# Sigmoid attention and mixture of depths on one core: the value matmuls from 32 rows to 64 rows

## The chip, the cores and the metric

The kernel runs on one core of a Trainium2 chip. The metric is device time in microseconds (us) of one execution; the time before is the median of three runs, 455.39 us (454.31 to 455.57). All data is float32.

## The reference

Two blocks follow each other. `q`, `k` and `v` are (8, 12, 448, 64): 8 batches, 12 heads, 448 tokens, 64 dimensions a head. The first block is attention with a sigmoid in place of the softmax; its output, heads side by side, is `x` (8, 448, 768). The second block picks 128 of the 448 tokens of each batch by a gate score and adds a gated two-layer network to those rows alone.

```python
scores = scale * np.matmul(q, k.transpose(0, 1, 3, 2)) - np.log(S)
attn = 1.0 / (1.0 + np.exp(-scores))
return np.matmul(attn, v).astype(np.float32)
...
scores = np.einsum('bsd,d->bs', x, w_gate)
out = x.copy()
for b in range(B):
    top_idx = np.argpartition(-scores[b], capacity)[:capacity]
    xe = x[b, top_idx]
    h = np.maximum(xe @ w1, 0.0)
    ye = h @ w2
    g = 1.0 / (1.0 + np.exp(-scores[b, top_idx]))
    out[b, top_idx] = x[b, top_idx] + g[:, None] * ye
```

`w1` is (768, 1024), `w2` is (1024, 768).

## The kernel before

**Quads, sets and slots.** Four heads of one batch are a quad; there are 24 quads and 12 sets `s` of two quads. The 448 tokens are 14 blocks of 32. A set has seven slots `n`; in slot `n` the keys of blocks `n` and `n + 7` (64 keys) are scored against all 448 queries, for both quads.

**Scores** (`score`, L329 to L341). VectorE has turned `q` and `k` in 32x32 squares, so that head `h` of a quad lies on the 32 partitions from `32 h` on, half of its 64 dimensions at a time (`e`). One matmul contracts 32 rows: the weights are 32x64 (64 keys), the moving operand is 32x448. It uses rows `32 h` of the array and, for quad `y` of the set, column half `y`. `pr` picks heads 0, 1 or heads 2, 3, so one call of `score` uses the lower or the upper two row groups, and both column halves. A pair of heads has its own PSUM tile `PA[pr]`, of two banks. ScalarE turns it into `attn[s, pr, n]` (`squash`, L352): 64 keys of the one quad on partitions 0 to 63, of the other on 64 to 127; the two heads of the pair side by side.

**Values** (`value`, L357 to L371). Here the keys are contracted. Before the change this is done by 32 rows: for quad `half` of a set, row group `2 half` holds one block of 32 keys and row group `2 half + 1` the other, and the output, the 64 dimensions of head `j` of pair `pr`, is added up in the bank `PO[x][pr]`. Two row groups that run at once write to different banks: with `p = 0` the lower row group does pair 0 and the upper one pair 1, with `p = 1` it is the other way round (`pr = r % 2 ^ p`). Each slot's blocks have to be done with both `p`. `rounds` (L717) lists which `p` and which two slots' blocks are done in the place of each slot; where `p` changes within a slot (`split`, L727), `join` (L373) lets ScalarE write one element into the banks between the two parts. In `rest` a `drain` stands between the two `p`.

**A slot** (`slot`, L737). Values lag four slots behind the scores. For `half` 0 and 1, with `pr = 1 - half`: first part of the scores (`e = 0`) of pair `pr`, the values of `half`, second part of the scores (`e = 1`), sigmoid. The scores of a half-slot so use one pair of row groups and its values the other pair. One half-slot before the change has 8 score matmuls and 8 value matmuls in the program; each float32 matmul leaves two weight loads and two matmuls in the trace. A split slot (L752 to L764) has both halves' values, then all scores, then both halves' values.

**Around the attention.** After slot 3 of a set, `after` (L851) brings: `load_v` (the values of a later set, four DMAs, L153), `block` (L679: a piece of the mixture-of-depths network for an earlier batch, as `BLOCKS` lists it, L649), `turn` (VectorE's 32x32 squares for `q` and `k`, L312, L320), `load`, `gates` (VectorE, L396, L399: two products and sums for each quad's part of the gate score). `takes` (L388) moves the finished values out of `PO` with VectorE. In `BLOCKS`, `("c", b)` is the choosing: small matmuls (L481, L485) that make the 128 token numbers of batch `b` out of `ranking` (L444 to L475, VectorE); `(1, p, key)` and `(2, p, key)` are products of the first and the second layer (L559, L623), with seven quarter products instead of eight; `("t", b)` turns the gathered rows (L523). Each item of a block takes its bank from the list `places`, whose first is a score bank and whose second is `PO[0][0]`. `RANKED` (L910) says after which slot a batch's `ranking` comes, `WEIGHTS` (L221) after which slot a quarter of `w1` or `w2` is loaded (768 KB each), `None` standing for the one that is kept in a spare tile.

**Order.** The program order is written out by hand. All loads and stores shown here are issued by SyncE's queue (SP) in that order; the gathers and scatters by GpSimd.

Of the kernel before, what the change touches and what calls it, by code (L numbers as in the profile page):

```python
# [17 lines left out]
def kernel(  # L18
# [11 lines left out]
    nc = tc.nc  # L30

    B, H, S, Dh = q.shape
# [4 lines left out]
    TT = 32  # L37
    TB = S // TT
    NF = 3
# [171 lines left out]
    def keep_sum(m, key):  # L211
# [6 lines left out]
            (6, 6): (2, 5), (7, 0): (2, 6), (7, 4): (2, 7), (7, 5): (2, 4)}  # L218
    KEPT = {(6, 0): [(1, 5), (1, 7)], (6, 1): [(1, 6)], (6, 5): [(1, 3)],
            (7, 0): [(2, 5)], (7, 1): [(2, 6)], (7, 5): [(2, 7)], (7, 6): [(2, 4)]}  # L220
    WEIGHTS = {(1, 2): (1, 0), (1, 5): (1, 1), (2, 1): (1, 2), (2, 2): (1, None),  # L221
               (5, 1): (2, 0), (5, 5): (2, 1), (6, 1): (2, 2), (6, 4): (2, None)}

    def attn_tile(pr, n):
# [129 lines left out]
    x_tiles, gate_parts, st = {}, {}, {}  # L354
    done = {}

    def value(s, half, p, n):  # L357


        for r in (2 * half, 2 * half + 1):  # L360
            x, c, step = chunks(s, n, half)
            pr = r % 2 ^ p
            rows = slice(r * TT, (r + 1) * TT)
            at = column(s, n, half) * Dh
            i = done[s, x, pr] = done.get((s, x, pr), 0) + 1
            for j in range(2):
                nc.tensor.matmul(PO[x][pr][j * Dh:(j + 1) * Dh, :S],  # L367
                                 raw_v[s][rows, 2 * pr + j, at:at + Dh],
                                 attn[s, pr, n][rows, j, :],
                                 start=((s, x, pr, j) not in done), stop=(i == TB))  # L370
                done[s, x, pr, j] = True  # L371

    def join(x):  # L373

# [266 lines left out]
    def scatter(b):  # L641
# [7 lines left out]
    BLOCKS = {  # L649
# [8 lines left out]
    }  # L658
# [20 lines left out]
    def block(s):  # L679

        places = [PA[1][:, 0], PO[0][0], PO[0][1], PA[0][:, 0], PO[1][0], PO[1][1], PA[0][:, 0]]
        work = BLOCKS.get(s, ())
        if work and work[0][0] == "c":
            chosen = choose(work[0][1], places.pop(0))
        takes(s - 1, 0)
        if work and work[0][0] == "c":
            fetch(*chosen)
            work = work[1:]
        takes(s - 1, 1)
        stores(s, NF)  # L690
        if s in FULL:
            gates(2 * s - 2)
        for item in work:
            if item[0] == "t":
                turn_rows(item[1], [places.pop(0) for _ in range(2)])
            elif item[0] == "c":
                fetch(*choose(item[1], places.pop(0)))
            else:
                finish(item, begin(item, places.pop(0)))
# [14 lines left out]
    outs = None  # L714
    FULL = [(NG * b + NG - 1) // 2 + 1 for b in range(B)]

    def rounds(s):  # L717


        if s == 0:  # L720
            return [(0, 0, 1), (1, 0, 1), (1, 0, 1), (0, 0, 1), (0, 4, 5), (0, 1, 6), (1, 4, 5)]
        same = [(0, 0, 1), (1, 0, 1), (1, 2, 3), (0, 2, 3), (0, 4, 5)]
        if s + 1 in BLOCKS:
            return same + [(1, 4, 5), (1, 0, 6)]
        return same + [(0, 1, 6), (1, 4, 5)]

    def split(s, i):  # L727
        return i == (6 if s + 1 in BLOCKS else 5)

    def entries(s, i, half):  # L730

        p, u, w = rounds(s)[i]
        if s == 0 and i < 4 and (i < 2) == bool(half):
            u, w = 2, 3
        return (p, u), (p, w)

    def slot(s, n):  # L737


        if s == 0 and n < NF + 1:  # L740
            if n == NF:
                first_outs.close()
                open_outs()
            psc = PA if n % 2 else outs
            for e in range(2):
                for pr in (1, 0):
                    score(s, n, e, pr, psc[pr])
            for pr in (1, 0):
                squash(s, n, pr, psc[pr])
            return  # L750
        vs, i = (s, n - NF - 1) if n > NF else (s - 1, n + NF)
        if split(vs, i):  # L752
            one, two, u = rounds(vs)[i]
            for half in range(2):
                value(vs, half, one, u)
                join(half)
            for e in range(2):
                for pr in (1, 0):
                    score(s, n, e, pr, PA[pr])
            for half in (1, 0):  # L760
                value(vs, half, two, u)
            for pr in (1, 0):
                squash(s, n, pr, PA[pr])
            return  # L764
        for half in range(2):
            pr = 1 - half
            a, b = entries(vs, i, half)
            if s == 0 and n == NF + 1 and half == 0:
                value(vs, half, *a)
                value(vs, half, *b)  # L770
                score(s, n, 0, pr, PA[pr])
            else:
                score(s, n, 0, pr, PA[pr])
                value(vs, half, *a)
                value(vs, half, *b)
            score(s, n, 1, pr, PA[pr])
            if vs == 0 and half == 1 and i in (1, 3):
                join(1 if i == 1 else 0)
            squash(s, n, pr, PA[pr])
            if i == 6 and s not in BLOCKS:  # L780
                takes(vs, half)

    def rest():


        s = NS - 1
        for p, some in ((1, (4, 5, 6)), (0, (2, 3, 4, 5, 6))):
            if p == 0:
                nc.tensor.drain()
            for n in some:  # L790
                for half in range(2):
                    value(s, half, p, n)
        for x in (0, 1):
            takes(s, x)
        gates(2 * NS - 2)
        p, b = NP - 2, B - 1
        turns[0] = 0
        work = [((1, p, 6), first(p, 6, bank()))]
        chosen = choose(b - 1, bank())
        work.append(((1, p, 7), begin((1, p, 7), bank())))  # L800
        gates(2 * NS - 1)
        fetch(*chosen)

        store(b, (0, 1))
        spread(b, nc.sync)
        store(b, (2, 3))
        for item, args in work:
            finish(item, args)
        for key in (4, 5):
            do((1, p, key))  # L810
        first_sums(*begin((1, p, 3), bank()), sums_too=(5, 6))
        work = {key: begin((2, p, key), bank()) for key in (2, 1, 4)}
        ranking(b)
        work[5] = begin((2, p, 5), bank())
        chosen = choose(b, bank())
        second_sums(*work[2])
        hidden_sum(p, 7)
        work[6] = begin((2, p, 6), bank())
        fetch(*chosen)
        second_sums(*work[1])  # L820
        hidden_sum(p, 3)
        work[7] = begin((2, p, 7), bank())
        for key in (4, 5, 6, 7):
            second_sums(*work[key])
        do(("t", b - 1))
        do((2, p, 3))
        p += 1
        for item in ((1, p, 1), ("t", b), (1, p, 2)):
            do(item)
        work = [((1, p, key), begin((1, p, key), bank())) for key in (3, 6, 7)]  # L830
        for item, args in work[1:]:
            finish(item, args)
        first_sums(*work[0][1], sums_too=())
        for key in (4, 5):
            do((1, p, key))
        for m in (5, 6, 7, 3):
            hidden_sum(p, m)
        for key in (1, 2, 6, 5, 3, 7, 4):
            do((2, p, key))
# [11 lines left out]
    def after(s, n):  # L851

        if n == NF and s:
            odd = s in FULL[1::2]
            if s > 4:
                load_v(s)
            if s in BLOCKS:
                block(s)
            else:
                stores(s, n)  # L860
                if s in FULL:
                    gates(2 * s - 2)
            if odd and s > 3:
                gates(2 * s - 1)
            turn("q", 2 * s + 2)
            turn("k", 2 * s + 3)
            load("k", 2 * s + 4)
            turn("q", 2 * s + 3)
            if s not in FULL:
                gates(2 * s - 2)  # L870
            if s == FIRST:
                ranking(1)
            if not odd or s == 3:
                gates(2 * s - 1)
        for m, key, place in LENT.get((s, n), ()):
            lend(m, key, place)
        if s == 0:
# [8 lines left out]
                load("k", 4)  # L886
            if n == 5:
                turn("q", 2, 3)
        if n == NF + 1 and 0 < s < 4:
            load_v(s + 1)  # L890
        if (s, n) in WEIGHTS:
            m, x = WEIGHTS[s, n]
            if x is None:
# [13 lines left out]
        if n != NF:  # L907
            stores(s, n)

    RANKED = [(3, 1), None, (6, 1), (7, 5), (9, 1), (10, 5), (11, 6)]  # L910

    first_outs = ExitStack()

# [58 lines left out]
```

## Time and profile before

One execution was profiled. Its own time was 459.74 us; its span, first to last instruction, 457.9 us.

| | before |
|---|---|
| median of three runs | 455.39 us |
| the profiled execution | 459.74 us |
| its span | 457.9 us |
| mean granted TensorE clock | 0.989 |
| VectorE busy | 302.2 us, 66% |
| ScalarE busy | 191.2 us, 42% |
| moved by DMA | 76.80 MB, mean 168 GB/s |

How to read it: PE is TensorE's matmuls, PEld its weight loads, DVE is VectorE, ACT ScalarE, POOL GpSimd, SP SyncE. In the names, `a` is a score bank, `o` a value bank, `x_b` the attention's output in SBUF, `xe` the gathered rows. The ends of matmuls are modelled, so their starts are what counts: the time from one start to the next on the same part of the array is what a matmul takes. "issue" is time in which an engine waited for nothing that the profile shows.

### The profile page before, as it was taken

How to read it: one execution, taken by the hardware profiler on the slowest of the kernel's cores; microseconds unless marked ns; L12 is line 12 of the kernel's file. 1: busy time of each engine (PE TensorE's matmuls, PEld its weight loads, DVE VectorE, ACT ScalarE, POOL GpSimd, SP SyncE). 2: the span in 40 equal slices, each digit the busy share in tenths (PEclk: the TensorE clock that was granted, in tenths of full speed). 3: DMA queues.
4: the chain of work that ended last, by engine and by line, in shares of the span. 5: the costliest groups of instructions: out<-in, count | busy, mean ns of one | idle time of the engine just before them, and what ended most of it. 6: DMA issues, size and time to landing. Idle time of an engine off the chain costs nothing.

```text
span 457.9 us, 14344 instructions
## 1 busy us (share of the span) xinstructions
PE 442.5 (97%) x6374; PEld 266.2 (58%) x6374; DVE 302.2 (66%) x639; ACT 191.2 (42%) x257; POOL 33.1 (7%) x55
## 2 busy tenths in 40 slices
PE   8999899799999999999999999999999999999994
PEld 3456554243437558556556758745544758769952
DVE  4316346692957997946898686653695688883372
ACT  3756456366564651551362462264165240102000
POOL 6000001000001000200001100110000100101001
PEclk9999999899999999999999999999999999999998
DMA  8972944989557789498866499369963985511001
GB/s 230 252 232 67 300 124 84 221 161 224 131 180 158 182 269 241 86 295 241 228 219 164 93 268 193 58 194 264 238 214 90 187 219 108 116 35 70 1 0 69
DMA packets 112846, 76.80 MB, mean 168 GB/s; under 512 B 90304, under 2 KB 99136, under 8 KB 112784
## 3 DMA queue, kind: packets, MB, share of 16 engines
q1 hardware_dynamic: 110800, 67.97, 58.6%
q0 software_dynamic: 1984, 7.91, 6.0%
q8 instruction: 50, 0.82, 0.8%
q14 instruction: 12, 0.10, 0.1%
HBM read 55.41 MB, written 20.46 MB: 166 GB/s over the span
## 4 chain that ended last, share of the span: by engine, by line
PE 90%; DVE 3%; ACT 3%; issue 2%; DMA 1%; POOLq 0%; ACTq 0%; DVEq 0%
PE a L338 30%; PE o L367 26%; PE o L623 11%; PE o L559 9%; PE a L559 7%; PE a L623 3%; ACT attn L352 2%; PE p L928 1%; ACT hidden L352 1%; DMA out_dram<-xe,idx 1%; DVE x_b L388 1%; PE o L523 1%; DVE scr L447 1%; DVE scr L444 1%; PE a L523 1%
## 5 line engine op out<-in xcount | busy, mean ns | idle before, releaser
L338 PE MATMUL a<-qT,kT 32*64 32x448 f32 x2624 | 249.0, 543 | 3.7 <-issue 2.9
L352 ACT ACTIVATE attn<-a,bias_s 128x896 f32<-128x896 f32 x162 | 161.9, 1007 | 103.2 <-PE a L338 99.3
L367 PE MATMUL o<-attn,raw_v 32*64 32x448 f32 x2176 | 200.1, 540 | 0.4 <-issue 0.3
L338 PEld LDWEIGHTS a<-qT,kT 32*64 32x64 f32 x2624 | 96.4, 132 | 98.9 <-ACT attn L352 53.6
L367 PEld LDWEIGHTS o<-attn,raw_v 32*64 32x64 f32 x2176 | 78.0, 132 | 30.2 <-issue 21.0
L388 DVE STREAM_TRANSPOSE x_b<-o 128x448 f32<-128x448 f32 x48 | 27.7, 623 | 60.2 <-PE o L367 39.3
L367 PE MATMUL o<-attn,rows_t 32*64 32x448 f32 x448 | 44.0, 560 | 1.4 <-issue 1.4
L575 ACT ACTIVATE hidden<-hidden 128x512 f32<-128x512 f32 x12 | 7.5, 630 | 63.6 <-DVE hidden L572 63.6
L320 DVE STREAM_TRANSPOSE kT<-raw_k 128x448 f32<-128x448 f32 x42 | 24.1, 613 | 13.4 <-DMA raw_k<-in_k_dram 12.7
L399 DVE TENSOR_REDUCE gate_p<-scr 128x14 f32<-128x448 f32 x48 | 29.8, 621 | 1.7
L396 DVE TENSOR_TENSOR scr<-x_b,wg_b 128x448 f32<-128x448 f32 x48 | 29.3, 611 | 1.0
L312 DVE STREAM_TRANSPOSE qT<-qT 128x896 f32<-128x896 f32 x23 | 25.0, 1087 | 5.2 <-DMA qT<-in_q_dram 5.1
L623 PE MATMUL o<-w_sb,hidden 128*128 128x384 f32 x80 | 27.3, 486 | 0.0
L634 DVE SCALAR_TENSOR_TENSOR xe<-o,gate,xe 128x384 f32<-128x384 f32 x36 | 20.5, 612 | 8.8 <-PE o L623 8.7
L367 PEld LDWEIGHTS o<-attn,rows_t 32*64 32x64 f32 x448 | 18.6, 136 | 7.9 <-issue 6.7
L447 DVE SCALAR_TENSOR_TENSOR scr<-rep,who,earlier 128x448 f32<-128x448 f32 (+1 forms) x32 | 21.9, 683 | 1.4
L559 PE MATMUL o<-rows_t,w_sb 128*128 128x128 f32 x192 | 22.7, 275 | 0.0
L572 DVE TENSOR_TENSOR hidden<-o,hidden 128x512 f32<-128x512 f32 x19 | 12.6, 687 | 14.8 <-PE o L559 14.5
L559 PEld LDWEIGHTS o<-rows_t,w_sb 128*128 128x128 f32 x192 | 22.2, 192 | 0.3
L444 DVE TENSOR_SCALAR_CACHE_REDUCE scr<-rep,who 128x448 f32<-128x448 f32 (+1 forms) x32 | 21.5, 673 | 1.0
L525 ACT ACTIVATE rows_t<-o 128x384 f32<-128x384 f32 x7 | 3.4, 482 | 44.3 <-PE o L523 44.3
L559 PEld LDWEIGHTS a<-rows_t,spare 128*128 128x128 f32 x168 | 19.3, 192 | 3.3 <-ACT attn L352 3.3
(114 smaller groups left out, 396.5 us busy)
## 6 DMA issues: line engine op xcount, KB each, us to landing
qT<-in_q_dram SPq DMA_DIRECT2D x24, 448.0 KB, 6.5
out_dram<-x_b SPq DMA_DIRECT2D x32, 336.0 KB, 7.9
raw_k<-in_k_dram SPq DMA_DIRECT2D x22, 448.0 KB, 4.7
raw_v<-in_v_dram SPq DMA_DIRECT2D x36, 224.0 KB, 5.3
spare<-sum SPq DMA_DIRECT2D x18, 384.0 KB, 6.2
sum<-spare SPq DMA_DIRECT2D x8, 768.0 KB, 6.0
w_sb<-in_moe_w_dram SPq DMA_DIRECT2D x6, 768.0 KB, 7.5
rows_t<-in_v_dram SPq DMA_DIRECT2D x8, 224.0 KB, 8.7
```

Of the source, the lines that this page charges most:

```text
L312: nc.vector.transpose(heads["q", i], heads["q", i])
L320: nc.vector.transpose(kt[:, e], t[:, e].rearrange("p (a n) d -> p n a d", a=2))
L338: nc.tensor.matmul(out[y * Dh:(y + 1) * Dh, h % 2, :S], kt[d, e, r:r + 2].rearrange("d r t -> d (r t)"), qt[d, e], start=(e == 0), stop=(e ...
L352: nc.scalar.activation(a, psc[:, :, :S], AF.Sigmoid, bias=bias_s, scale=QK_SCALE)
L367: nc.tensor.matmul(PO[x][pr][j * Dh:(j + 1) * Dh, :S], raw_v[s][rows, 2 * pr + j, at:at + Dh], attn[s, pr, n][rows, j, :], start=((s, x, p ...
L388: nc.vector.transpose(x_tiles[b][:, :, 2 * g + pr, :], PO[x][pr][:, :S].rearrange("p (r t) -> p r t", t=TT))
L396: nc.vector.tensor_tensor(out=tmp, in0=x_tiles[b][:, :, hp, :], in1=wg_b[:, hp:hp + 1, :].to_broadcast([P, TB, TT]), op=ALU.mult)
L399: nc.vector.tensor_reduce(out=gate_parts[b][:, :, hp], in_=tmp, axis=AX.X, op=ALU.add)
L444: nc.vector.tensor_scalar(out=junk[:n], in0=rep[:n], scalar1=own, scalar2=0.0, op0=ALU.is_gt, op1=ALU.add, accum_out=above[:n, c:c + 1])
L447: nc.vector.scalar_tensor_tensor(out=junk[:n], in0=rep[:n], scalar=own, in1=earlier[:n, c, :], op0=ALU.is_equal, op1=ALU.mult, accum_out=l ...
L559: nc.tensor.matmul(ps[:, f, :n], w((t * FH + f) * P, P), x[:, t, :n], start=(t == 0), stop=(t == KH - 1))
L623: nc.tensor.matmul(ps[:n, :DH], h[:, t, :n], w(t * DH, DH), start=(t == 0), stop=(t == FH - 1))
```

## The change

`value` contracts 64 rows in one matmul: both blocks of 32 keys of a quad are added up inside the array, and the two pairs are done one after the other in the same rows. The weights become 64x64 and the moving operand 64x448. `rounds`, `split` and `entries` go, and with them the split slot; each slot place now does the values of one slot (`entry`). The drain in `rest` goes.

Beside it: `load_v` of sets 2 to 4 moves from after slot 4 to after slot 3, ahead of that slot's other loads; two of the weight loads move from after slots (2, 1) and (2, 2) to after (1, 6) and (4, 4); in the blocks of sets 6 and 9 the choosing moves from the end to the front; in sets 3, 6 and 9 the gates come after the turns; two rankings come one slot later.

```diff
-    WEIGHTS = {(1, 2): (1, 0), (1, 5): (1, 1), (2, 1): (1, 2), (2, 2): (1, None),
+    WEIGHTS = {(1, 2): (1, 0), (1, 5): (1, 1), (1, 6): (1, 2), (4, 4): (1, None),
...
-    def value(s, half, p, n):
-        for r in (2 * half, 2 * half + 1):
-            x, c, step = chunks(s, n, half)
-            pr = r % 2 ^ p
-            rows = slice(r * TT, (r + 1) * TT)
-            at = column(s, n, half) * Dh
-            i = done[s, x, pr] = done.get((s, x, pr), 0) + 1
+    def value(s, half, n):
+        x, c, step = chunks(s, n, half)
+        rows = slice(half * Dh, (half + 1) * Dh)
+        at = column(s, n, half) * Dh
+        i = done[s, x] = done.get((s, x), 0) + 1
+        for pr in range(2):
             for j in range(2):
                 nc.tensor.matmul(PO[x][pr][j * Dh:(j + 1) * Dh, :S],
                                  raw_v[s][rows, 2 * pr + j, at:at + Dh],
                                  attn[s, pr, n][rows, j, :],
-                                 start=((s, x, pr, j) not in done), stop=(i == TB))
-                done[s, x, pr, j] = True
+                                 start=(i == 1), stop=(i == NU))
...
-        6: [(1, 0, 6), (1, 0, 7), (1, 0, 4), (1, 0, 5), (2, 0, 1), ("c", 2)],
+        6: [("c", 2), (1, 0, 6), (2, 0, 1), (1, 0, 7), (1, 0, 4), (1, 0, 5)],
...
-        9: [(1, 1, 6), (1, 1, 7), (1, 1, 4), (1, 1, 5), (2, 1, 1), ("c", 4)],
+        9: [("c", 4), (1, 1, 6), (2, 1, 1), (1, 1, 7), (1, 1, 4), (1, 1, 5)],
...
-        if s in FULL:
+        if s in FULL[::2]:
             gates(2 * s - 2)
...
+    def entry(s, i, half):
+        if s == 0 and i < 4:
+            return i ^ 2 if half else i
+        return i
...
-        if split(vs, i):
-            one, two, u = rounds(vs)[i]
-            for half in range(2):
-                value(vs, half, one, u)
-                join(half)
-            for e in range(2):
-                for pr in (1, 0):
-                    score(s, n, e, pr, PA[pr])
-            for half in (1, 0):
-                value(vs, half, two, u)
-            for pr in (1, 0):
-                squash(s, n, pr, PA[pr])
-            return
         for half in range(2):
             pr = 1 - half
-            a, b = entries(vs, i, half)
-            if s == 0 and n == NF + 1 and half == 0:
-                value(vs, half, *a)
-                value(vs, half, *b)
-                score(s, n, 0, pr, PA[pr])
-            else:
-                score(s, n, 0, pr, PA[pr])
-                value(vs, half, *a)
-                value(vs, half, *b)
+            first_values = s == 0 and n == NF + 1 and half == 0
+            if first_values:
+                value(vs, half, entry(vs, i, half))
+            score(s, n, 0, pr, PA[pr])
+            if not first_values:
+                value(vs, half, entry(vs, i, half))
             score(s, n, 1, pr, PA[pr])
...
-        for p, some in ((1, (4, 5, 6)), (0, (2, 3, 4, 5, 6))):
-            if p == 0:
-                nc.tensor.drain()
-            for n in some:
-                for half in range(2):
-                    value(s, half, p, n)
+        for n in range(3, NU):
+            for half in range(2):
+                value(s, half, n)
...
         if n == NF and s:
-            odd = s in FULL[1::2]
             if s > 4:
                 load_v(s)
+            elif s < 4:
+                load_v(s + 1)
             if s in BLOCKS:
                 block(s)
             else:
                 stores(s, n)
-                if s in FULL:
-                    gates(2 * s - 2)
-            if odd and s > 3:
-                gates(2 * s - 1)
+            if s == 2:
+                gates(2 * s - 2)
             turn("q", 2 * s + 2)
             turn("k", 2 * s + 3)
             load("k", 2 * s + 4)
             turn("q", 2 * s + 3)
-            if s not in FULL:
+            if s not in FULL[::2]:
                 gates(2 * s - 2)
             if s == FIRST:
                 ranking(1)
-            if not odd or s == 3:
-                gates(2 * s - 1)
+            gates(2 * s - 1)
...
-        if n == NF + 1 and 0 < s < 4:
-            load_v(s + 1)
...
-    RANKED = [(3, 1), None, (6, 1), (7, 5), (9, 1), (10, 5), (11, 6)]
+    RANKED = [(3, 1), None, (6, 1), (7, 6), (9, 1), (10, 6), (11, 6)]
```

More of the change, by code (lines that the diff above doesn't have):

```diff
@@ L715 @@
     FULL = [(NG * b + NG - 1) // 2 + 1 for b in range(B)]
[L717 to L735, printed above, removed]
+    def entry(s, i, half):
+        if s == 0 and i < 4:
+            return i ^ 2 if half else i
+        return i
     def slot(s, n):
```

## The prediction, made before the result was known

> **What bounds the kernel now.** I read the page's busy shares first, then its chain of waits, then its groups, then PE's timeline in three places, because a busy PE says nothing of how much of the array works.
>
> ```profile
> PE 442.5 (97%) x6374; PEld 266.2 (58%) x6374; DVE 302.2 (66%) x639; ACT 191.2 (42%) x257; POOL 33.1 (7%) x55
> ...
> PE 90%; DVE 3%; ACT 3%; issue 2%; DMA 1%; POOLq 0%; ACTq 0%; DVEq 0%
> ...
> L338 PE MATMUL a<-qT,kT 32*64 32x448 f32 x2624 | 249.0, 543 | 3.7 <-issue 2.9
> ...
> L367 PE MATMUL o<-attn,raw_v 32*64 32x448 f32 x2176 | 200.1, 540 | 0.4 <-issue 0.3
> ```
>
> 90% of the chain is PE's own work, half of it scores (L338) and values (L367). Whatever PE does in one slot of the 84 counts. The timeline of an ordinary half-slot says how full the array is:
>
> ```profile
> 120.01 0.55 PE L338 MATMUL a<-qT,kT 32*64 32x448 f32 x4
> 120.04 0.56 PE L367 MATMUL o<-attn,raw_v 32*64 32x448 f32 x4
> 120.39 0.55 PE L338 MATMUL a<-qT,kT 32*64 32x448 f32 x4
> 120.42 0.91 PE L367 MATMUL o<-attn,raw_v 32*64 32x448 f32 x8
> 120.80 0.56 PE L338 MATMUL a<-qT,kT 32*64 32x448 f32 x4
> 121.15 0.55 PE L367 MATMUL o<-attn,raw_v 32*64 32x448 f32 x4
> ```
>
> Every 0.376 us (120.01 to 120.39) four scores and four values start together: eight 32x64 tiles, the whole array. A half-slot has 16 + 16 records, four such rounds, 1.50 us; a slot 3.01. Measured from the ends of its sigmoids (L352), an ordinary slot lasts 3.01 to 3.04 us. So there is nothing left to win inside an ordinary slot; there is only something to lose.
>
> **The value matmuls.** The streaming work stays. A half-slot's values were 8 matmuls (16 records) on four 32x64 tiles, four records each; now they are 4 matmuls (8 records) on two 64x64 tiles, four records each: again four rounds of 0.376 us, beside four rounds of scores in the other half of the rows. This holds if a 64-row and a 32-row matmul can share the array for nothing. No row of this trace has two shapes at once. The nearest are the places where the shape changes, between 128 rows and 32:
>
> ```profile
> 146.52 0.27 PE L523 MATMUL a<-iden,xe 128*128 128x128 f32 x1
> 146.72 0.60 PE L338 MATMUL a<-qT,kT 32*64 32x448 f32 x4
> 146.75 0.60 PE L367 MATMUL o<-attn,raw_v 32*64 32x448 f32 x4
> 147.15 0.55 PE L338 MATMUL a<-qT,kT 32*64 32x448 f32 x4
> ```
>
> Within one shape a 128x128 matmul follows the last after 0.11 us (24 of L559 in 2.68 us on the chain). Here the next starts after 0.20, and its own first round takes 0.43 (146.72 to 147.15) in place of 0.376. A change of shape costs 0.09 + 0.05 = 0.14 us, without any wait on a semaphore. In the new kernel each half of the rows goes from scores (32) to values (64) or back once in each half-slot. 80 slots have both (3 in set 0, 7 in each of 11 sets), so 160 half-slots x 0.14 = 22.4 us.
>
> Bounds: below, 0, if only 128 rows do this (the two shapes of now, scores and values, are the same 32x64, and passing from one to the other costs nothing). Above, if the wait is for the whole array and not for the rows concerned: then values run alone, four rounds, 1.50 us, and only the second scores of one pair and the first of the next (neighbours in the program, in different rows) still run together, two rounds, 0.75 us, with two changes, 0.28: 2.53 us a half-slot for 1.50, 160 x 1.03 = 165 us. I take 22.4, since the order of the program (scores of `pr = 1 - half` around the values of `half`) leaves the rows disjoint, and the row seen is a price for each change.
>
> The Trainium skill, TensorEngine Tiling (Array Packing), Key Properties, speaks against this change: a change of tiling mode, not just of tile, drains TensorE. By that rule the upper bound would hold and the sum be about 165 us worse; by the rows above the rule agrees with 0.14 us at each change, but they cannot say whether other rows must drain too.
>
> **Split slot and drain.** Slot 3 of sets 5 to 11 is split and lasts 3.09 to 3.13 us, some 0.1 above the others: 11 of these, -1.0 us (0 to -1.2). In the tail the drain shows as one gap of 0.64 us between value matmuls in place of 0.376: -0.3 us.
>
> **Fewer instructions, and where weights are loaded.** Two long gaps of PE wait for nothing shown:
>
> ```profile
> 51.45 1.23 PE L367 MATMUL o<-attn,rows_t 32*64 32x448 f32 x6
> 54.08 0.59 PE L367 MATMUL o<-attn,rows_t 32*64 32x448 f32 x2 [1.40 <-issue]
> ```
>
> ```profile
> 81.59 0.91 PE L338 MATMUL a<-qT,kT 32*64 32x448 f32 x2
> 85.44 1.44 PE L338 MATMUL a<-qT,kT 32*64 32x448 f32 x16 [2.94 <-issue]
> ```
>
> In the DMA records the queue that loads code (50 loads, 0.82 MB) had one at 39.99 us and the next at 51.51, another at 69.27 and the next at 82.67, where the others of the attention come every 5 to 7 us; the DMA engines were full then, the first time behind the two 768 KB loads that SP issued at 49.93 and 50.40 (396 GB/s from 52 to 58). PE ran out of code. Start to start the gaps are 1.94 and 3.47 us, less 0.38 of work each 1.6 and 3.1; after each the granted clock is 0.5 for 3.41 us (from 55.17 and 85.89), another 1.7 each. Together 3.3 and 4.8 us. The change takes those two weight loads away from there, and a slot has 96 PE instructions for 128, so a load of code lasts 8 us of slots for 6. I take the first gap as gone and half of the second: -5.7 us. Bounds: both gone, -8.1; a new gap of the second's size elsewhere, since (1, 6) gets a 768 KB load, +4.8.
>
> **Choosing first, in sets 6 and 9.** In set 6 VectorE is late:
>
> ```profile
> 168.93 2.94 PE L559 MATMUL a<-rows_t,spare 128*128 128x128 f32 x24
> 172.10 0.38 PE L559 MATMUL o<-rows_t,spare 128*128 128x128 f32 x1 [0.23 <-DVE x_b L388]
> ```
>
> PE reaches the block at 168.93 and has one product to do in a score bank while VectorE ends the sums of batch 2 (171.40) and moves out the values (L388). With the choosing first that product comes after, in `PO[0][0]`: PE waits to about 171.5, does the choosing (0.43 us, as from 182.83 to 183.26) and starts the product at about 172.1 with nothing done: 2.7 us lost, 0.4 won back at the block's end, +2.3. In set 9 VectorE's sums end at 276.4 and PE arrives at 278.3: only the wait for the first L388, +0.4. If slots are 0.28 us longer (two changes), VectorE gains 2.0 us on PE over the seven slots from (5, 4) to (6, 3) and the 2.3 shrink to 0.3: +0.7 in all. If they are not, +2.7.
>
> **At nothing:** gates after turns, and two rankings one slot later: VectorE idles 34% and rankings of (7, 6) and (10, 6) have four slots, 12 us, for some 10 us of VectorE; without that cover the next block's choosing waits some 2 us. `load_v` first in sets 1 to 3: its four DMAs (1.8 to 2.2 us of SP at 42.80 and 74.20) go past SP's store and the load of `k`, whose reader, `turn` at the next set's slot 0, comes 12 us later; `k` lands in 4.7 us. If `k` is late, scores of the set after are late, up to 4 us (VectorE already waited 4.3 us for one `k` load about 85 us).
>
> **Sum**, from the profiled execution's 459.74: +22.4 - 1.0 - 0.3 - 5.7 + 0.7 = 475.8. That execution is 4.35 above the median of the runs, so 475.8 - 4.35 = **471.5 us**.
>
> **Rivals.** (1) *The shapes share the array for nothing.* For it: today's kernel passes between scores and values without a price, on all eight tiles. Against: every change of shape in the trace costs 0.14 us. Then 459.74 - 1.0 - 0.3 - 5.7 + 2.7 - 4.35 = 451.1: faster. It decides as soon as a change costs under 0.03 us (4.3 / 160). (2) *The whole array drains* at each change, and values never run beside scores: 471.5 + 165 - 22.4 = 614. For it: after the last 128-row matmul no 32-row tile starts early, and no row shows two shapes at once. Against it: with 128 rows all tiles overlap, so these rows would look the same if only the rows concerned had to wait. (3) *Free sharing, but the code gap moves*: the load at (1, 6) or `load_v` first starves PE once more, 451.1 + 5.7 + 4.8 = 461.6; for it the DMA engines, full from 44 to 58 us; against it the fewer instructions.
>
> **Chances.** Forecast 0.57, its own range 460 to 488 (0.07 to 0.23 us a change, with the bounds of the code gaps). Rival 1 0.28 (447 to 456), rival 2 0.08, rival 3 0.07. The range from 448 to 490 leaves out rival 2 and the ends of the others. About 0.3%, 1.4 us, is what a measurement of this kernel can tell from no change. Faster by more than that: most of rival 1, 0.24; same: its upper end, 0.04; slower: the rest, 0.72.
>
> **What would show it.** Rounds of L367 with 64 rows beside L338 at 0.376 us, and 0.43 to 0.52 at the passage, slots of 3.3 us: the forecast. Slots of 3.0: rival 1; of 5: rival 2, with no L338 and L367 starting together. Gaps of "issue" over 1 us tell of the code; PE's wait ahead of L481 in set 6 tells of the choosing. Wrong would make it a change of shape that costs another price than the passage from 128 rows.

## The result, and the profile after

The changed kernel takes 648.57 us (median of 4 runs, 646.83 to 651.22), the kernel before, on the same chip, 454.85 us (453.73 to 455.57): a ratio of 1.4267, 95% interval [1.4205, 1.433]. The profiled execution after has a span of 645.9 us, for 457.9 before. The forecast was 471.5; what came is rival 2 (614), and some 35 us on top of it.

From the page of the changed kernel: busy shares, the granted clock in 40 slices, the chain by engine, and the two groups of the attention.

```profile
PE 634.2 (98%) x5030; PEld 259.2 (40%) x5030; DVE 306.0 (47%) x639; ACT 187.8 (29%) x213; POOL 32.7 (5%) x55
...
PEclk9999999999655559999999999999999999999998
...
PE 96%; DMA 2%; issue 0%; DVE 0%; ACT 0%; SPq 0%; POOLq 0%; DVEq 0%
...
L366 PE MATMUL o<-attn,raw_v 64*64 64x448 f32 x1088 | 247.3, 590 | 0.0
L338 PE MATMUL a<-qT,kT 32*64 32x448 f32 x2624 | 184.0, 593 | 0.4 <-DVE got L493 0.4
```

PE looks as busy as before (98% for 97%), with 1344 matmul records fewer. The busy share hides that the array is half empty while values run; two lines point to the loss. The scores' records are as many as before, but their busy time fell from 249.0 to 184.0 us, since they now run in bursts, eight at a time, where four ran beside four values; and the clock row has a hole five slices long. The timeline shows how (PE alone, set 3, start and length in us):

```profile
150.38 1.01 PE L338 MATMUL a<-qT,kT 32*64 32x448 f32 x16
151.31 1.72 PE L366 MATMUL o<-attn,rows_t 64*64 64x448 f32 x8
152.97 1.01 PE L338 MATMUL a<-qT,kT 32*64 32x448 f32 x16
153.90 1.72 PE L366 MATMUL o<-attn,rows_t 64*64 64x448 f32 x8
155.55 1.01 PE L338 MATMUL a<-qT,kT 32*64 32x448 f32 x16
```

No score starts while values run, though they use other rows. A period is 16 score records (the second scores of one pair and the first of the next), 0.93 us from start to start, and 8 value records, 1.66 us: 2.59 us a half-slot where it was 1.50. Ordinary slots last 5.18 us, measured as before from the ends of the sigmoids, for 3.02.

**Where the 188 us between the two spans went** (the medians are 194 apart). Sets 1 to 11 have 69 slots without a block behind them and 8 with one; set 0 has three with values.

| | us |
|---|---|
| 72 slots x (5.18 - 3.02) | +155.5 |
| 8 slots with a block, about 1.6 each (set 8: 16.29 to 17.88) | +13 |
| a stretch at half clock, 164.8 to 239.9 us (sized below) | +33 |
| sets 1 to 3 over 21 slots of 3.02 before (22.94 + 26.40 + 27.45 us: the code gaps, their half clocks, slow slots), gone after | -13.4 |
| sum | +188 |

The third row is not the change of shape itself. At the choosing of set 4 PE has a thin stretch, and the clock then stays at half for 75 us (PE of the changed kernel; then what the windows of that trace give: length, busy us and number of instructions of PE, PEld, DVE, ACT and POOL, granted clock, DMA share, GB/s):

```profile
160.73 0.98 PE L338 MATMUL a<-qT,kT 32*64 32x448 f32 x8
161.64 1.05 PE L483 MATMUL a<-who,hot 128*128 128x2 f32 x8
163.08 0.98 PE L338 MATMUL a<-qT,kT 32*64 32x448 f32 x8 [0.39 <-DVE got L493]
164.00 2.52 PE L366 MATMUL o<-attn,raw_v 64*64 64x448 f32 x8
```

```profile
168.00:200.00 32.00, 32.00 (x160) 7.28 (x152) 11.50 (x27) 7.05 (x7) 0.00 (x0) 0.50 0.28 96
200.00:236.00 36.00, 36.00 (x174) 10.55 (x171) 3.36 (x8) 8.12 (x10) 0.97 (x1) 0.50 0.15 34
```

PE is busy for every one of these 68 us, at a granted clock of 0.50; a slot lasts 9.81 us there. The stretch ends in the block of set 5, 4.8 us after its first full-array products start (235.1 to 239.9). In the kernel before, the clock came back 3.41 us after each of the two long gaps of PE.

### The profile page after: what moved, and what is told of

The parts are those of the page before. It is cut to its first block, busy times and chain, and to the rows that moved or that the text cites. A ratio compares the mean times of both kernels' runs of the same rounds, so it can differ in the third digit from the quotient of the medians.

```text
span 645.9 us, 11631 instructions
## 1 busy us (share of the span) xinstructions
PE 634.2 (98%) x5030; PEld 259.2 (40%) x5030; DVE 306.0 (47%) x639; ACT 187.8 (29%) x213; POOL 32.7 (5%) x55
## 4 chain that ended last, share of the span: by engine, by line
PE 96%; DMA 2%; issue 0%; DVE 0%; ACT 0%; SPq 0%; POOLq 0%; DVEq 0%
PE o L366 45%; PE a L338 26%; PE o L621 8%; PE o L557 7%; PE a L557 5%; PE a L621 2%; DMA qT<-in_q_dram 1%; PE o L521 1%; DMA out_dram<-xe,idx 0%; PE a L483 0%; PE a L521 0%; PE a L479 0%; ACT attn L352 0%; PE p L338 0%; PE o L483 0%
## 5 line engine op out<-in xcount | busy, mean ns | idle before, releaser
L352 ACT ACTIVATE attn<-a,bias_s 128x896 f32<-128x896 f32 x162 | 163.1, 1007 | 290.6 <-PE a L338 285.1
L366 PE MATMUL o<-attn,raw_v 64*64 64x448 f32 x1088 | 247.3, 590 | 0.0
L338 PE MATMUL a<-qT,kT 32*64 32x448 f32 x2624 | 184.0, 593 | 0.4 <-DVE got L493 0.4
L366 PEld LDWEIGHTS o<-attn,raw_v 64*64 64x64 f32 x1088 | 67.2, 140 | 170.2 <-issue 158.0
L386 DVE STREAM_TRANSPOSE x_b<-o 128x448 f32<-128x448 f32 x48 | 30.2, 642 | 168.7 <-PE o L366 167.1
L338 PEld LDWEIGHTS a<-qT,kT 32*64 32x64 f32 x2624 | 42.0, 135 | 125.8 <-issue 125.0
L366 PE MATMUL o<-attn,rows_t 64*64 64x448 f32 x224 | 48.2, 549 | 0.0
L366 PEld LDWEIGHTS o<-attn,rows_t 64*64 64x64 f32 x224 | 13.3, 132 | 32.9 <-issue 29.7
L570 DVE TENSOR_TENSOR hidden<-o,hidden 128x512 f32<-128x512 f32 x21 | 13.9, 688 | 24.9 <-PE o L557 24.8
L557 PE MATMUL o<-rows_t,spare 128*128 128x128 f32 x168 | 20.0, 277 | 0.0
L503 POOL DMA_INDIRECT xe<-out_dram,idx x7 | 7.0, 1001 | 247.2 <-DVE got L493 168.2
```

What stands on the lines that cost most here:

```text
L338: nc.tensor.matmul(out[y * Dh:(y + 1) * Dh, h % 2, :S], kt[d, e, r:r + 2].rearrange("d r t -> d (r t)"), qt[d, e], start=(e == 0), stop=(e ...
L352: nc.scalar.activation(a, psc[:, :, :S], AF.Sigmoid, bias=bias_s, scale=QK_SCALE)
L366: nc.tensor.matmul(PO[x][pr][j * Dh:(j + 1) * Dh, :S], raw_v[s][rows, 2 * pr + j, at:at + Dh], attn[s, pr, n][rows, j, :], start=(i == 1), ...
L386: nc.vector.transpose(x_tiles[b][:, :, 2 * g + pr, :], PO[x][pr][:, :S].rearrange("p (r t) -> p r t", t=TT))
L557: nc.tensor.matmul(ps[:, f, :n], w((t * FH + f) * P, P), x[:, t, :n], start=(t == 0), stop=(t == KH - 1))
```

## The experiments

Theory: a change of tile shape makes the whole array wait, so two shapes never run together (rival 2 of the prediction). Against it: that a 64-row matmul is slow in itself; that only the rows concerned wait; that the new order of loads and choosing has a part. Ratios are to the kernel before, run on the same chip in the same session.

**1. The order and the values apart.** `order_only` keeps `value`, `rounds` and `split` of before and takes every other edit; `value_only` takes the new `value`, `entry` and `slot` and keeps the order of before.

```diff
  order_only, against the kernel before:
+    WEIGHTS = {(1, 2): (1, 0), (1, 5): (1, 1), (1, 6): (1, 2), (4, 4): (1, None),
+        6: [("c", 2), (1, 0, 6), (2, 0, 1), (1, 0, 7), (1, 0, 4), (1, 0, 5)],
+        9: [("c", 4), (1, 1, 6), (2, 1, 1), (1, 1, 7), (1, 1, 4), (1, 1, 5)],
...
+            elif s < 4:
+                load_v(s + 1)
...
  value_only, against the kernel after: the same lines put back
```

> The kernel before with all the edits of order (loads of v first, weights, choosing first, gates, rankings) and the value matmuls as before, 32 rows. If the loss is all in the 64-row matmuls: 450 to 460 us, slots of 3.0 us. If the new order costs part of it: over 470.

> The kernel after with the order of before (loads, weights, choosing, gates, rankings) and 64-row values. If the whole loss is in the value matmuls: slots of 5.18 us, 610 to 655 us, the higher end if the clock again falls to half for some 75 us. If the order has a part: clearly under 610.

Measured: `order_only` 456.07 us, ratio 1.0047 [0.9996, 1.0098]; `value_only` 646.8 us, 1.4249 [1.4182, 1.4317], slots of 5.18 us, half clock for 71.7 us. The whole loss is in the value matmuls; the order has no part that can be told from nothing, and below two of its parts turn out to be a gain and a loss that nearly cancel.

**2. Fewer changes of shape.** `grouped` does all scores of a slot, then all values: two changes in place of four, same 64-row matmuls.

```diff
+        for e in range(2):
+            for pr in (1, 0):
+                score(s, n, e, pr, PA[pr])
+        for half in range(2):
+            value(vs, half, entry(vs, i, half))
...
+        for pr in (1, 0):
+            squash(s, n, pr, PA[pr])
```

> The kernel after with all four score calls of a slot first and then both halves' values: two changes of shape a slot in place of four, each shape filling all rows. If a change of shape makes the whole array wait: 4 + 4 rounds of 0.376 and two changes of 0.16, 3.3 us, plus 0.3 to 0.5 for the second sigmoid, a slot of 3.6 to 3.9 us, 500 to 535 us. If 64-row matmuls are slow in themselves (the two halves of the rows can't run values together): slots of 4.9 us or more, over 590 us.

Measured: 491.51 us, ratio 1.0831 [1.0783, 1.0879]. The 64-row matmuls are not slow: with both halves of the rows at values, 16 records take what 8 took alone (PE of `grouped`):

```profile
92.13 2.12 PE L338 MATMUL a<-qT,kT 32*64 32x448 f32 x32
94.18 1.75 PE L366 MATMUL o<-attn,raw_v 64*64 64x448 f32 x16
95.86 1.82 PE L338 MATMUL a<-qT,kT 32*64 32x448 f32 x32
97.61 0.62 PE L366 MATMUL o<-attn,raw_v 64*64 64x448 f32 x4
```

Values last 1.68 us (94.18 to 95.86): four rounds of 0.376 and a change. Slots alternate between 3.4 and 3.75 us, a mean of 3.58, a little under what was expected. The shorter is near the bare sum of eight rounds and two changes (3.3); that the second sigmoid makes the longer one is what the order suggests, and was not tried by itself. The same work costs 157 us less than in the kernel after, 33 of them for the long half clock that doesn't occur.

**3. The price of one change, in the kernel before.** `probe64` adds one tiny matmul of 64 rows and a single column in 66 ordinary slots; `probe32` adds the same with 32 rows, the shape that scores and values have.

```diff
+            if half == 0 and s:
+                nc.tensor.matmul(PA[pr][:Dh, 0, S:S + 1], iden[:Dh, :Dh], iden[:Dh, :1],
+                                 start=True, stop=True)
  probe32: iden[2 * TT:3 * TT, :Dh], iden[2 * TT:3 * TT, :1]
```

> The kernel before with one added matmul in each of 66 ordinary slots of sets 1 to 11, of 64 rows and 64 columns and a single moving column, ahead of the first scores. If a change of shape makes the whole array wait: each costs two changes of 0.14 us and the offset between the two halves of the rows, 0.3 to 0.8 us, 475 to 508 us. If only the rows concerned wait, or only long matmuls: under 0.15 us each, under 465 us.

> The same added matmul with 32 rows, the shape of scores and values, in the same 66 places: the control. If it is the shape that costs: under 0.1 us each, 453 to 461 us. If it is the added instruction and its place in the queue: as the run with 64 rows.

Measured: `probe64` 471.17 us, 1.0363 [1.0325, 1.0401]; `probe32` 458.93 us, 1.0096 [1.0053, 1.0139]. The control lies where it was expected. The 64-row probe lies 4 us below its range, and far above the 0.15 us a slot of the other theory: 16.3 us over 66 slots are 0.25 each. In the traces an ordinary slot lasts 3.40 us with 64 rows, 3.12 with 32, 3.02 without: the instruction itself costs 0.10, the two changes of shape 0.28, that is 0.14 each. At 0.38 a slot 66 slots would give 25 us. They give less because the eight slots with a block lose nothing, as the shape changes there anyway (set 8: 16.29 us before, 16.30 here), and because some waits of the kernel before are shorter here (slot (7, 0): 3.83 before, 3.37 here). PE of `probe64`:

```profile
71.42 0.56 PE L367 MATMUL o<-attn,raw_v 32*64 32x448 f32 x4
71.45 0.55 PE L338 MATMUL a<-qT,kT 32*64 32x448 f32 x4
71.93 0.27 PE L769 MATMUL a<-iden 64*64 64x1 f32 x2
72.14 0.60 PE L338 MATMUL a<-qT,kT 32*64 32x448 f32 x4
72.16 0.60 PE L367 MATMUL o<-attn,raw_v 32*64 32x448 f32 x4
```

Here is the answer to what the trace of before could not say. The added matmul uses the lower half of the rows. In each slot one half of the rows is at scores and the other at values, and both stop for it: no record of either starts between 71.45 and 72.14, and then both start together, 0.21 us after the added matmul. That this is not just its place in the queue shows the control, whose added matmul lies in rows 64 to 95: there scores start 0.02 us after it (66.54 and 66.56 us in its trace). The whole array waits, not the rows concerned.

**4. Is it the rows?** `columns32` is the kernel before with each value matmul split into two of 32 columns: 32 rows as the scores have, another width.

```diff
-                nc.tensor.matmul(PO[x][pr][j * Dh:(j + 1) * Dh, :S],
-                                 raw_v[s][rows, 2 * pr + j, at:at + Dh],
+                for d in range(0, Dh, TT):
+                    nc.tensor.matmul(PO[x][pr][j * Dh + d:j * Dh + d + TT, :S],
+                                     raw_v[s][rows, 2 * pr + j, at + d:at + d + TT],
```

> The kernel before with each value matmul split into two of 32 rows by 32 columns (same work for each tile, twice the value instructions); scores stay 32x64. If any change of tile shape, columns too, makes the whole array wait: half-slots of 2.6 us, 600 to 660 us. If only a change in the number of rows does: half-slots of 1.5 us, 455 to 480 us with more code to load.

Measured: 638.76 us (a single execution), with the timeline of the kernel after (PE of `columns32`):

```profile
110.40 1.01 PE L338 MATMUL a<-qT,kT 32*64 32x448 f32 x16
111.34 1.73 PE L368 MATMUL o<-attn,raw_v 32*32 32x448 f32 x32
113.00 1.01 PE L338 MATMUL a<-qT,kT 32*64 32x448 f32 x16
113.94 1.73 PE L368 MATMUL o<-attn,raw_v 32*32 32x448 f32 x32
```

2.60 us a half-slot. A difference in columns alone keeps two matmuls apart as a difference in rows does.

**5. The half clock.** `filled` puts six full-array matmuls (128x128x512, result not read) behind the choosing of set 4; `late_fill` puts eight of them after slot (4, 5), some 15 us into the stretch at half clock.

```diff
+            if s == 4:
+                for _ in range(6):
+                    nc.tensor.matmul(PA[1][:, 1], w1_sb[:, 0, :P], w1_sb[:, 0, :512],
+                                     start=True, stop=True)
  late_fill: in after(), if (s, n) == (4, 5), eight of them
```

> The kernel after with six added matmuls of 128x128x512 behind the choosing of set 4 (5.1 us of full-array work whose result nobody reads). If the half clock from 165 to 240 us starts with PE's thin stretch at that choosing and lasts only because a half-filled array does not end it: no such stretch, about 648.6 - 36 + 5 = 618 us. If the alternating shapes themselves bring the clock down: still some 70 us at half clock, 650 us.

> The kernel after with eight added matmuls of 128x128x512 after slot (4, 5), some 15 us into the stretch at half clock (7 us at full clock, 14 at half; nobody reads the result). If that stretch lasts only because the alternating, half-filled array does not end it, and full-array work does: the clock is 1.0 again soon after them, near 190 us, some 45 us earlier; 25 us saved and 9 us of added work, about 630 us. If the clock follows something else (time, the block of set 5): half clock to about 250 us and 655 to 660 us.

Measured: `filled` 620.26 us, 1.3651 [1.3593, 1.3709], clock 1.0 from 15.9 to 616.7 us in its trace (span 618.8), 33.4 us less than the kernel after once its 5.1 us of added work are taken off; one of its four runs took 659.28 us at a mean clock of 0.935, and has no trace. The window of `filled` where the kernel after was at half clock:

```profile
170.00:200.00 30.00, 29.71 (x274) 8.17 (x276) 16.66 (x36) 10.22 (x11) 1.05 (x1) 1.00 0.39 128
```

`late_fill` 632.75 us, 1.3922 [1.3844, 1.3999], half clock for 23.9 us in place of 75 (windows of `late_fill`, columns as above):

```profile
164.00:180.00 16.00, 16.00 (x78) 3.73 (x76) 13.62 (x30) 3.02 (x3) 0.00 (x0) 0.50 0.32 102
180.00:190.00 10.00, 10.00 (x24) 3.40 (x21) 0.00 (x0) 1.01 (x1) 0.00 (x0) 0.64 0.00 0
190.00:200.00 10.00, 10.00 (x78) 2.88 (x84) 1.17 (x2) 2.01 (x2) 0.00 (x0) 1.00 0.08 16
```

The clock returned at 187.3 us, 4.4 us after the added matmuls began (182.93), and stayed at 1.0 through the same alternating slots that had not brought it back. So in three of four runs of `filled` full-array work right behind the thin work at the choosing kept the stretch away, and in `late_fill` such work ended it; the alternating, half-filled array can hold a full clock, but did not win it back. `grouped` supports this from another side: its shapes alternate too, but each fills the array, and its clock fell to 0.5 at 39.2 us, behind a wait of 1.64 us, and came back after 6.8 us with no work of 128 rows between.

**6. The order's gain and loss.** Four versions of the kernel before, each with a part of the new order.

```diff
  weights_only
+    WEIGHTS = {(1, 2): (1, 0), (1, 5): (1, 1), (1, 6): (1, 2), (4, 4): (1, None),
  vfirst_only
+            elif s < 4:
+                load_v(s + 1)
-        if n == NF + 1 and 0 < s < 4:
-            load_v(s + 1)
  loads_only: both; choose_first: the lines of BLOCKS for sets 6 and 9
```

> The kernel before with two edits of order alone: the two weight loads in their new slots and the loads of v first. If PE's gaps near 52 and 82 us come of full DMA engines that delay its code, as the run of all the order edits suggests (set 3 ended 7.8 us earlier): 445 to 451 us, faster than before. If the early gain is given back later for any reason: 453 to 457 us.

> The kernel before with the loads of v of sets 2 to 4 after slot 3 alone, the weights where they were. If the second gap of PE (82 us) comes of these loads' place: 2 to 5 us less than before, the gap near 52 us still there. If the weights alone make the gain: as before.

> The kernel before with the two weight loads after (1, 6) and (4, 4) alone. If the gap near 52 us comes of them: it goes, 3 us less than before, the one near 82 us stays. If the gain is made by the loads of v: as before.

> The kernel before with the choosing at the front of the blocks of sets 6 and 9 alone. If PE waits in set 6 for VectorE's sums of batch 2, as worked out in the prediction: +2.3 and +0.4 us, and +1.7 more if that wait drops the clock for 3.41 us: 456 to 460 us. If VectorE is early enough: 453 to 456 us.

| | median us | ratio, 95% interval |
|---|---|---|
| `loads_only` | 451.63 | 0.9936 [0.9901, 0.9971] |
| `vfirst_only` | 450.66 | 0.9896 [0.9853, 0.9939] |
| `weights_only` | 454.37 | 0.9996 [0.9962, 1.003] |
| `choose_first` | 457.46 | 1.0063 [1.0029, 1.0097] |

The gain is the loads of v, not the weights: `vfirst_only` beats both kernels, the one before by 4.7 us (ratio x 455.55, the median of the kernel before in its session). Its windows from 52 to 58 us and 82 to 88 us, where the kernel before had its gaps and mean clocks of 0.76 and 0.82:

```profile
52.00:58.00 6.00, 6.00 (x128) 2.84 (x128) 0.00 (x0) 4.36 (x8) 0.00 (x0) 1.00 0.90 312
82.00:88.00 6.00, 6.00 (x120) 3.15 (x110) 5.83 (x13) 3.48 (x4) 0.00 (x0) 1.00 0.87 174
```

PE runs through both, though the two weight loads still stand at the first place. SP issues the v of set 3 at 60.43 us there, in place of 74.20. The queue that loads code follows: around the second gap its loads come at 69.27 and 82.67 us before, at 67.18, 72.95 and 79.73 with the loads of v first, and still 11 to 12 us apart in `weights_only` (66.28, 78.08) and `choose_first` (64.57, 75.92), which leave the loads of v alone. With the weights moved alone the gaps are shorter (1.24 us from start to start near 51.5, 1.87 near 79) but still there.

The gaps differ from trace to trace, though, also where the loads are as before. In `choose_first` slot (2, 1) lasts 3.24 us where the profile of before has 6.66, slot (3, 2) 5.08 for 8.08, and no half clock follows either; in `probe32` and `probe64` slot (3, 2) lasts 3.13, without a gap. The profile of before, 459.74 us for a median of 454.85, shows both at their longest. So one trace cannot say which edit closed a gap, the one near 52 us above all; that the loads of v are worth 4.7 us rests on the times.

`choose_first` loses 2.9 us (ratio x 455.55; the medians are 1.9 apart). In set 6 PE waits for VectorE's sums, as worked out (the last columns of its PE line: idle before, and what ended it):

```profile
164.44 0.38 PE L481 MATMUL a<-ones,sums 128*128 128x1 f32 x2 [0.91 <-DVE sums L472]
```

Its slot with the block of set 6 lasts 19.85 us, for 18.74 before and 18.25 in `weights_only`; that of set 9 lasts 18.19 for 18.25, so no loss is seen there. With all edits of order together two such waits show (PE of `order_only`), each with 3.41 us at half clock behind it:

```profile
162.20 0.35 PE L481 MATMUL a<-ones,sums 128*128 128x1 f32 x2 [1.28 <-DVE sums L472]
218.28 1.25 PE L367 MATMUL o<-attn,raw_v 32*64 32x448 f32 x6 [2.27 <-DMA raw_v<-in_v_dram]
```

The second, for a load of v in set 7, lasts 0.17 us in `choose_first`. The gates and the two rankings were not run by themselves, so which edit makes it longer stays open.

## Why the prediction was wrong, point by point

- **What bounds the kernel.** Right: PE at eight tiles, 3.01 us a slot, nothing to win inside a slot. That left all the risk on the one question of the shapes.
- **The price of a change of shape, 0.14 us.** Right, from rows of 128 against 32: `probe64` gives 0.14 for 64 against 32. In the changed kernel the two changes of a half-slot come to 0.33 (2.59 less six rounds of 0.376), 0.17 each.
- **The step that failed: "I take 22.4, since the order of the program (scores of `pr = 1 - half` around the values of `half`) leaves the rows disjoint".** The wait is for the whole array, and disjoint rows don't help. The upper bound of that step, 2.53 us a half-slot and 165 us, measured 2.59 us and 168 us (155.5 + 13). I let the pairing of the rows in the program decide how the chip behaves, which it can't: the pairing serves the kernel before as well, where all tiles have one shape.
- **The skill's rule.** TensorEngine Tiling (Array Packing), Key Properties, has it that a change of tiling mode drains TensorE. It was right, and it was the only source that told the two bounds apart; the runs agree with 0.14 us and a stop of all rows at each change. By the rule the forecast would have been 142.6 us higher, since the 165 replaces the 22.4 and is not added to it. I gave rival 2 a chance of 0.08; with two bounds that no row could choose between, it should have had the larger share.
- **Missing from every rival: the clock.** 33 us of the loss are a stretch at half clock. The profile of before had the first half of it, a drop to 0.5 after each of the two long gaps of PE; that a half-filled array would not end it was in no row.
- **Split slot and drain, -1.3 us.** Not seen by themselves; the new slots are longer by more than the split cost. The term was also read too small: the split slots of sets 1 to 3 last 3.56 to 3.62 us, not 3.09 to 3.13, which makes it up to 2.5 us in place of 1.0. From the last sigmoid of set 11 to PE's last matmul the trace after is 0.9 us shorter (76.65 for 77.57), which is all that the drain and the last values can have brought.
- **Code gaps, -5.7 us.** The size was about right, the cause half wrong: I gave the first gap to the weight loads and left the loads of v as an edit at nothing. The loads of v make the whole gain (-4.7 us by themselves); the weights make none that can be told. That the size came out is in part luck: both gaps were sized in an execution that shows them longer than any other trace, and the 4.35 us by which it exceeds the median were taken off as well, so part of them was probably counted twice.
- **Choosing first, +0.7 (or +2.7 without longer slots).** The second figure is the one for the kernel before, and measured 2.9 (1.3 to 4.4 by the interval). The 0.4 of it that was for set 9 is not seen.
- **The range, 448 to 490.** It left out rival 2 on purpose. A bound that no row excludes, seven times the value taken, belongs in the range or needs an experiment's worth of reasons against it.

## What to carry to other kernels

In all pairs tried here, tiles of the PE array ran side by side only if all had the same shape: before merging small matmuls into a larger one, look at what runs beside them. If two shapes are needed, group each (here 491.5 us for 648.6) and count 0.14 to 0.17 us for each passage. And a busy PE says nothing of how full the array is: count the records that start together.

## What the runs showed of the hardware that was not expected

- A change of tile shape stopped all rows and columns, also for a difference in columns alone (`columns32`: 2.60 us a half-slot for 1.50) and for a matmul of a single column (`probe64`: 0.28 us for going there and back).
- The granted clock fell to 0.50 after about 1.5 us of thin work (161.6 to 163.1 us) and stayed there for 75 us with PE busy throughout; full-array work brought it back 4.4 us after it began (`late_fill`, at 187.3 us). With nothing else changed, filling the array at one place saved 33.4 us in three runs of four, beside the 5.1 us that the filling took.
- The place of loads in SP's queue seems to move the loads of PE's code: with the v of set 3 issued at 60.43 us in place of 74.20, the pause of 13.4 us between two loads of code (69.27 to 82.67) was 6.8 at most (72.95 to 79.73). Moving the loads of v of three sets forward by one slot was worth 1.0% (0.9896 [0.9853, 0.9939]).
